# Expert blocks of 640 slots with wide matmuls and unordered scatters, beside a bias MLP computed by matrix products per row group: one change to an attention and mixture-of-experts kernel

## The chip, the cores and the metric

The kernel runs on one core of a Trainium2 chip. The metric is the device time of one execution in microseconds (us); times of several runs are given by their median. Engines: TensorE (PE, with its weight loads PEld), VectorE (DVE), ScalarE (ACT), GpSimd (POOL) and SyncE (SP); DMA transfers are issued here from SP's queue and from POOL's.

## What is computed

Attention over 8 batches and 8 heads, 576 positions of 64 numbers, with a bias that a small MLP (1 to 32 to 8) makes from the relative position; the bias does not depend on the batch. The result, seen as 4608 rows of 512, then goes through a two-layer MLP (512 to 1024 to 512), one of eight experts for each row, as `domain_id` says.

```
scores = scale * q @ k.T
rel = |i - j|;  x = log1p(rel) / log1p(max(i, 1))
bias = relu(x * w1 + b1) @ w2                 # [576, 576, 8 heads]
attn = softmax(scores + bias);  y = attn @ v
x = y as [4608, 512]
for e in range(8):
    rows = (domain_id == e)
    out[rows] = relu(x[rows] @ w1[e]) @ w2[e]
```

The inputs are drawn with a fixed seed. The eight experts get 566, 557, 545, 612, 562, 561, 618 and 587 rows.

## The kernel before

The work stands in five parts, one after the other in the program: constants, bias, routing, attention, experts. A scheduler fixes the order of the instructions on each engine when the kernel is built; an engine then runs its instructions strictly in that order, each after the semaphores it waits for. Tiles come from pools, and a pool closed before another is opened gives its memory to the next, so that the first writers of the new tiles wait for the last readers of the old ones.

*Constants* (`_setup_constants`). The argument of the bias MLP is a log of |i - j| divided by a log of i. One table `L4` holds log1p of the distance for all shifts, with the four groups of 32 partitions one step apart, and `slope` holds w1 / log1p(i) for each row: a row group of four positions i is then one DVE operation that reads a shifted window of 576 columns of `L4` (f16 in SBUF), multiplies by a column of `slope`, and takes the maximum with `nb1`, which is -b1 (L108).

*Bias* (`_phase_fire`). Nine bands of 64 positions. Each band makes 16 tiles `hr` (L108) with forty buffers, then 80 small matmuls (L119) with `hr` as weights against `W2BIG` (32 columns) into the PSUM tile `eb`, which holds two chunks of columns and has four buffers. ACT takes each `eb` out with exp and stores it, with the heads moved outward, into `biasall` (L125). The biases are thus kept as factors exp(bias).

*Routing* (`_phase_route`). A one-hot of the domains, prefix sums along the columns, one matmul for the sum over partitions (`app`), and the slot of each row (`posi`): expert times 768 plus its rank. 36 indirect DMAs from POOL (L190) scatter the row numbers to `fire_perm` in DRAM, 128 each, and each waits for the one before it, since they write the same tensor. SP reads the table back as `permE`; empty slots are filled with the number of the first row of the tile, giving `gidx`.

*Attention* (`_phase_attention`). Per batch POOL issues the casting loads of q (L221) and k (L224). Per head: 18 transposes on PE, two DVE copies to `qkT`, v loaded on SP (L246, L248) and cast on POOL to `vext`, the scores `sc` (L274), exp on ACT (L278), the product with `biasall` on DVE (L284). Then `pu` (L295), normalised by DVE (L300, L301) and written to `fire_x` in DRAM by SP (L307).

*Experts* (`_phase_moe`). Per expert two casting weight loads (L316, L319), 1 MB each in SBUF, two buffers; then six tiles of 128 slots. A tile is gathered by an indirect DMA (L323, two buffers), transposed (L328), copied (L331), goes through 32 matmuls of 128 columns (L335), relu on ACT (L340), 8 matmuls of 512 columns (L343), a copy to `res` (L346, two buffers), and an indirect DMA that scatters the rows to the output (L347). The scatters write one tensor and keep their order.

Of the kernel before, what the change touches and what calls it, by code (L numbers as in the profile page):

```python
# [24 lines left out]
E = 8  # L25
CAP = 768
NCH = CAP // 128
NTOK = B * S
NGR = S // 4
LC = S - 4  # L30
LW = LC + S

# [17 lines left out]
def _setup_constants(tc, G, w1, b1, w2):  # L50

    nc = tc.nc
    cst = G.cst
    G.idn = cst.tile([P, P], F16, tag="idn", name="idn")  # L60
    make_identity(nc, G.idn)

    w1col = cst.tile([P, 1], F32, tag="w1col", name="w1col")
    nc.sync.dma_start(out=w1col, in_=bass.AP(tensor=w1.tensor, offset=0, ap=[[0, 4], [1, 32], [1, 1]]))
    G.nb1 = cst.tile([P, 1], F32, tag="nb1", name="nb1")
    nc.sync.dma_start(out=G.nb1, in_=bass.AP(tensor=b1.tensor, offset=0, ap=[[0, 4], [1, 32], [1, 1]]))
    nc.vector.tensor_scalar(out=G.nb1, in0=G.nb1, scalar1=-1.0, scalar2=None, op0=AO.mult)
    w2sb = cst.tile([HID, 8], F32, tag="w2sb", name="w2sb")
    nc.sync.dma_start(out=w2sb, in_=w2[:, :])
    G.W2BIG = cst.tile([P, 32], F16, tag="W2BIG", name="W2BIG")  # L70
    nc.gpsimd.memset(G.W2BIG, 0.0)
    for g in range(4):
        nc.vector.tensor_scalar(
            out=G.W2BIG[32 * g: 32 * g + 32, 8 * g: 8 * g + 8],
            in0=w2sb, scalar1=8.0, scalar2=None, op0=AO.mult,
        )

    si = cst.tile([P, NGR], I32, tag="si", name="si")
    li = cst.tile([P, LW], I32, tag="li", name="li")
    for g in range(4):  # L80
        nc.gpsimd.iota(si[32 * g: 32 * g + 32, :], base=g, channel_multiplier=0, pattern=[[4, NGR]])
        nc.gpsimd.iota(li[32 * g: 32 * g + 32, :], base=-(LC + g), channel_multiplier=0,
                       pattern=[[1, LW]])
    G.slope = cst.tile([P, NGR], F32, tag="slope", name="slope")
    nc.vector.tensor_copy(out=G.slope, in_=si)
    nc.vector.tensor_scalar(out=G.slope, in0=G.slope, scalar1=1.0, scalar2=None, op0=AO.max)
    nc.scalar.activation(out=G.slope, in_=G.slope, func=AF.Ln, bias=1.0, scale=1.0)
    nc.vector.reciprocal(out=G.slope, in_=G.slope)
    nc.vector.tensor_scalar(out=G.slope, in0=G.slope, scalar1=w1col[:], scalar2=None, op0=AO.mult)
    lf = cst.tile([P, LW], F32, tag="lf", name="lf")  # L90
    nc.vector.tensor_copy(out=lf, in_=li)
    nc.vector.scalar_tensor_tensor(out=lf, in0=lf, scalar=-1.0, in1=lf, op0=AO.mult, op1=AO.max)
    G.L4 = cst.tile([P, LW], F16, tag="L4", name="L4")
    nc.scalar.activation(out=G.L4, in_=lf, func=AF.Ln, bias=1.0, scale=1.0)

    G.biasall = cst.tile([P, NJC, 8, S], F16, tag="biasall", name="biasall")


def _phase_fire(tc, G):
    nc = tc.nc  # L100
    with tc.tile_pool(name="fsb", bufs=1) as fsb, \
         tc.tile_pool(name="fps", bufs=1, space=bass.MemoryType.PSUM) as fps:
        for ib in range(S // 64):
            hrl = []
            for k16 in range(16):
                m = 16 * ib + k16
                hr = fsb.tile([P, S], F16, tag="hr", name="hr", bufs=40)
                nc.vector.tensor_scalar(out=hr, in0=G.L4[:, LC - 4 * m: LC - 4 * m + S],  # L108
                                        scalar1=G.slope[:, m: m + 1], scalar2=G.nb1[:],
                                        op0=AO.mult, op1=AO.max)  # L110
                hrl.append(hr)
            for jcs in ((0, 1), (2, 3), (4,)):
                n = len(jcs)
                jw = JC[jcs[0]][1]
                eb = fps.tile([P, 2, 512], F32, tag="eb", name="eb", bufs=4)
                for k16 in range(16):
                    for lj, jc in enumerate(jcs):
                        j0 = JC[jc][0]
                        nc.tensor.matmul(  # L119
                            out=eb[0:jw, lj, 32 * k16: 32 * k16 + 32],  # L120
# [4 lines left out]
                nc.scalar.activation(  # L125
                    out=G.biasall[0:jw, jcs[0]: jcs[0] + n, :, 64 * ib: 64 * ib + 64],
                    in_=eb[0:jw, 0:n, :].rearrange("p l (i h) -> p l h i", h=8),
                    func=AF.Exp, bias=0.0, scale=0.125)


def _phase_route(tc, G, moe_domain_id):
    nc = tc.nc
    perm_dram = nc.dram_tensor("fire_perm", (E * CAP, 1), I32, kind="Internal").ap()
# [18 lines left out]
    ut = pbuf.tile([P, P], F16, tag="ut", name="ut")  # L152
    nc.gpsimd.memset(ut, 1.0)
    nc.gpsimd.affine_select(out=ut, in_=ut, compare_op=AO.is_ge, fill=0.0,
                            base=-1, channel_multiplier=-1, pattern=[[1, P]])
    apref = pbuf.tile([P, 8, 1], F32, tag="apref", name="apref")
    with tc.tile_pool(name="pps", bufs=1, space=bass.MemoryType.PSUM) as pps:
        app = pps.tile([P, 8], F32, tag="app", name="app")
        nc.tensor.matmul(out=app, lhsT=ut, rhs=rowtot16, start=True, stop=True)
        nc.vector.tensor_copy(out=apref, in_=app.unsqueeze(-1))  # L160
    pa = pbuf.tile([P, 8, 80], F32, tag="pa", name="pa")
# [5 lines left out]
    for sh in (1, 2, 4, 8, 16, 32):  # L167
# [6 lines left out]
    etile = pbuf.tile([P, 8, 36], F32, tag="etile", name="etile")  # L174
    nc.vector.tensor_scalar(out=etile, in0=rap(eif, 0, [[1, 8], [0, 36]]),
                            scalar1=float(CAP), scalar2=None, op0=AO.mult)
    nc.vector.tensor_tensor(out=rtile, in0=rtile, in1=etile, op=AO.add)
# [6 lines left out]
    neg48 = pbuf.tile([P, 48], I32, tag="neg48", name="neg48")  # L184
    nc.gpsimd.memset(neg48, -1)
    nc.sync.dma_start(out=perm_dram.rearrange("(p c) o -> p (c o)", c=48), in_=neg48)
    nidx = pbuf.tile([P, 36], I32, tag="nidx", name="nidx")
    nc.gpsimd.iota(nidx, base=0, channel_multiplier=1, pattern=[[128, 36]])
    for c in range(36):
        nc.gpsimd.indirect_dma_start(  # L190
            out=perm_dram[:, :],
            out_offset=bass.IndirectOffsetOnAxis(ap=posi[:, c:c + 1], axis=0),
            in_=nidx[:, c:c + 1], in_offset=None)
    permE = pbuf.tile([P, E * NCH, 1], I32, tag="permE", name="permE")
    nc.sync.dma_start(out=permE, in_=bass.AP(tensor=perm_dram.tensor, offset=0,
                                             ap=[[1, 128], [128, E * NCH], [1, 1]]))
    permEf = pbuf.tile([P, E, NCH], F32, tag="permEf", name="permEf")
    nc.vector.tensor_copy(out=permEf, in_=permE.rearrange("p (e kk) o -> p e (kk o)", e=E))
    mneg = pbuf.tile([P, E, NCH], F32, tag="mneg", name="mneg")
    nc.vector.tensor_scalar(out=mneg, in0=permEf, scalar1=0.0, scalar2=-1.0,  # L200
                            op0=AO.min, op1=AO.mult)
    tsel = pbuf.tile([P, E, NCH], F32, tag="tsel", name="tsel")
    nc.vector.tensor_tensor(out=tsel, in0=permEf[:, :, 0:1].to_broadcast([P, E, NCH]),
                            in1=mneg, op=AO.mult)
    nc.vector.tensor_tensor(out=tsel, in0=tsel, in1=mneg, op=AO.add)
    nc.vector.tensor_tensor(out=permEf, in0=permEf, in1=tsel, op=AO.add)
    G.gidx = pbuf.tile([P, E, NCH], I32, tag="gidx", name="gidx")
# [200 lines left out]
```

## Time and profile before

| | us |
|---|---|
| median of 11 runs (lowest, highest) | 683.79 (678.13, 694.79) |
| the profiled execution | 684.41 |
| its span | 682.2 |
| busy: PE, PEld | 512.1 (75%), 354.4 (52%) |
| busy: DVE, ACT, POOL | 357.4 (52%), 248.5 (36%), 253.4 (37%) |
| bias stage, from the first L108 to the last L119 | 12.4 to 68.2 |
| first score matmul to the last write of `fire_x` | 85.1 to 416.2 |
| first expert matmul to the last row scatter | 433.9 to 678.2 |

The span is the time from the first to the last instruction that the profiler saw; the time of the execution has 2.2 us around it. Busy shares are means over stages with very different limits. In a group of the profile the columns are the line, the engine, the operation, what it writes and reads with shapes and count, then busy us, mean ns of one, and the idle time of the engine just before with what ended it.

The chain of work that ended last has DMA 31%, PE 29%, ACT 12%, DVE 10%, POOL 6% of the span, and 11% in which an engine waited for nothing that the profile shows. By line, the row scatters of the experts have 18%, the permutation scatters 5%, L274 9%, L278 8%, L119 6%.

### The profile page before, as it was taken

Reading aid. Unit: us, or ns where it says so; the run is one execution under the profiler, and the core shown is the slowest. Engines: PE = TensorE matmul, PEld = TensorE weight load, DVE = VectorE, ACT = ScalarE, POOL = GpSimd, SP = SyncE. Lnnn points to the kernel's source line nnn. Section 1 sums busy time; section 2 is a strip of 40 time slices with the busy share of each in tenths; the row PEclk is TensorE's granted clock in tenths of the full one; section 3 lists DMA queues with packets and bytes.
Section 4 is the critical chain, followed back from the end, with each engine's and each line's share of the span. In section 5 each row is a group of like instructions: output and inputs, shape, how many; then the busy total and the mean of one; then the engine's idle time right before and its main releaser. Section 6 shows DMA issues by size and latency. Waiting matters only on the chain.

```text
span 682.2 us, 15154 instructions
## 1 busy us (share of the span) xinstructions
PE 512.1 (75%) x6225; PEld 354.4 (52%) x6225; DVE 357.4 (52%) x948; ACT 248.5 (36%) x271; POOL 253.4 (37%) x508
## 2 busy tenths in 40 slices
PE   2888197876987538778787873598879697969795
PEld 1777155545555326464555543465646465646463
DVE  6996476785767547868697882121212221212121
ACT  2433175380763713827374560122121121212121
POOL 4000644664744704222230402244435253443442
PEclk9999999797559957977898796699798998979899
DMA  1000999219294393791930205939293847667521
GB/s 4 2 2 1 117 93 101 66 29 121 54 66 76 41 66 89 57 102 37 98 78 20 70 1 106 199 101 186 92 186 98 182 107 164 132 148 149 136 94 61
DMA packets 149292, 60.32 MB, mean 88 GB/s; under 512 B 127720, under 2 KB 140520, under 8 KB 149224
## 3 DMA queue, kind: packets, MB, share of 16 engines
q0 software_dynamic: 93824, 45.12, 53.1%
q1 hardware_dynamic: 55400, 14.25, 10.8%
q8 instruction: 48, 0.79, 0.5%
q14 instruction: 20, 0.16, 0.1%
HBM read 68.22 MB, written 17.34 MB: 125 GB/s over the span
## 4 chain that ended last, share of the span: by engine, by line
DMA 31%; PE 29%; ACT 12%; issue 11%; DVE 10%; POOL 6%; POOLq 0%; SPq 0%; DVEq 0%; ACTq 0%
DMA out_dram<-res,gidx 18%; PE sc L274 9%; ACT eT L278 8%; PE eb L119 6%; DMA fire_perm<-nidx,posi 5%; PE pu L295 5%; PE ops L343 4%; DVE eT L284 4%; DMA fire_x<-xt 3%; DMA xg<-fire_x,gidx 3%; ACT biasall L125 2%; PE hps L335 2%; POOL xg L323 2%; DVE xt L301 2%; PE ptk L237 2%
## 5 line engine op out<-in xcount | busy, mean ns | idle before, releaser
L278 ACT ACTIVATE eT<-sc 128x1152 f16<-128x1152 f32 (+1 forms) x192 | 173.7, 965 | 162.7 <-PE sc L274 161.9
L274 PE MATMUL sc<-qkT 128*128 128x512 f16 (+5 forms) x640 | 130.1, 337 | 27.7 <-DVE qkT L242 15.4
L284 DVE TENSOR_TENSOR eT<-eT,biasall 128x576 f16<-128x576 f16 (+1 forms) x320 | 135.3, 469 | 25.9 <-ACT eT L278 25.2
L346 DVE COPY res<-ops 128x512 f32<-128x512 f32 x48 | 33.2, 691 | 184.5 <-PE ops L343 120.1
L340 ACT ACTIVATE hsb<-hps 128x1024 f16<-128x1024 f32 x48 | 49.1, 1023 | 218.3 <-PE hps L335 187.7
L335 PEld LDWEIGHTS <-w1e 128*128 128x128 f16 x1536 | 94.9, 100 | 21.0 <-issue 10.8
L343 PE MATMUL ops<-w2e,hsb 128*128 128x512 f16 x384 | 99.5, 406 | 7.5 <-ACT hsb L340 6.7
L335 PE MATMUL hps<-xgT,w1e 128*128 128x128 f16 x1536 | 100.6, 223 | 5.7 <-DVE xgT L331 5.3
L295 PE MATMUL pu<-vext,eT 128*128 128x65 f16 (+1 forms) x1600 | 75.2, 207 | 35.9 <-DVE xt L301 14.5
L347 POOL DMA_INDIRECT out_dram<-res,gidx x48 | 47.4, 986 | 126.8 <-DMA out_dram<-res,gidx 76.4
L295 PEld LDWEIGHTS <-eT 128*128 128x128 f16 (+1 forms) x1600 | 65.9, 110 | 48.0 <-DVE xt L301 20.8
L274 PEld LDWEIGHTS <-qkT 128*128 128x128 f16 (+1 forms) x640 | 52.7, 111 | 64.6 <-issue 26.8
L249 POOL CAST vext<-vf 128x256 f16<-128x256 f32 x64 | 30.4, 475 | 97.8 <-PE pu L295 77.6
L343 PEld LDWEIGHTS <-hsb 128*128 128x128 f16 x384 | 36.1, 103 | 53.7 <-ACT hsb L340 14.7
L119 PE MATMUL eb<-W2BIG,hr 128*128 128x32 f16 (+1 forms) x720 | 48.1, 199 | 20.1 <-DVE hr L108 12.9
L323 POOL DMA_INDIRECT xg<-fire_x,gidx x48 | 46.8, 975 | 24.8 <-issue 12.3
L190 POOL DMA_INDIRECT fire_perm<-nidx,posi x36 | 38.3, 1064 | 45.7 <-DMA fire_perm<-nidx,posi 38.5
L119 PEld LDWEIGHTS <-hr 128*128 128x128 f16 (+1 forms) x720 | 40.1, 112 | 28.0 <-DVE hr L108 12.9
L234 PE MATMUL ptq<-idn,q 64*64 64x64 f16 x576 | 41.0, 206 | 13.8 <-DMA q<-in_q_dram 8.3
L234 PEld LDWEIGHTS <-q 64*64 64x64 f16 x576 | 30.3, 119 | 37.2 <-issue 26.5
L328 PE MATMUL pxt<-idn,xg 128*128 128x128 f16 x192 | 17.1, 238 | 42.6 <-DMA xg<-fire_x,gidx 42.5
L108 DVE TENSOR_SCALAR hr<-L,slope,nb 128x576 f16<-128x576 f16 x144 | 49.0, 421 | 0.0
(70 smaller groups left out, 356.1 us busy)
## 6 DMA issues: line engine op xcount, KB each, us to landing
vf<-in_v_dram SPq DMA_DIRECT2D x64, 128.0 KB, 2.3
w1e<-in_moe_w_dram POOLq DMA_DIRECT2D x8, 1024.0 KB, 9.2
w2e<-in_moe_w_dram POOLq DMA_DIRECT2D x8, 1024.0 KB, 12.6
q<-in_q_dram POOLq DMA_DIRECT2D x8, 576.0 KB, 8.7
k<-in_k_dram POOLq DMA_DIRECT2D x8, 576.0 KB, 10.2
fire_x<-xt SPq DMA_DIRECT2D x32, 128.0 KB, 1.8
vf<-in_v_dram SPq DMA_DIRECT2D x64, 16.0 KB, 2.1
xg<-fire_x,gidx POOLq DMA_INDIRECT x48, 3.3
```

Of the source, the lines that this page charges most:

```text
L108: nc.vector.tensor_scalar(out=hr, in0=G.L4[:, LC - 4 * m: LC - 4 * m + S], scalar1=G.slope[:, m: m + 1], scalar2=G.nb1[:], op0=AO.mult, op ...
L119: nc.tensor.matmul(out=eb[0:jw, lj, 32 * k16: 32 * k16 + 32], lhsT=hrl[k16][:, j0: j0 + jw], rhs=G.W2BIG[:, 0:32], start=True, stop=True,)
L234: nc.tensor.transpose(out=ptq[:, 64 * m: 64 * m + 64], in_=q16[0:64, g9, :], identity=G.idn[0:64, 0:64])
L274: nc.tensor.matmul(out=po, lhsT=qkT[:, 1, j0: j0 + jw], rhs=qkT[:, 0, i0s: i0s + iwd], start=True, stop=True)
L278: nc.scalar.activation(out=eT[0:jw0, jgl: jgl + njc, :], in_=sc[0:jw0, 0:njc, :], func=AF.Exp, bias=0.0, scale=scale)
L284: nc.vector.tensor_tensor(out=eT[0:jw, jcn, :], in0=eT[0:jw, jcn, :], in1=G.biasall[0:jw, jcn, h, :], op=AO.mult)
L295: nc.tensor.matmul(out=pu[0:icw, hq, 0:65], lhsT=eTs[h][:, jcn, ic0: ic0 + icw], rhs=vexts[h][:, jcn, 0:65], start=(jcn == 0), stop=(jcn = ...
L323: nc.gpsimd.indirect_dma_start(out=xg[:], out_offset=None, in_=x_dram[:], in_offset=bass.IndirectOffsetOnAxis(ap=G.gidx[:, e, kk: kk + 1], ...
L335: nc.tensor.matmul(out=hps[:, 128 * fc: 128 * fc + 128], lhsT=w1e[:, dc, 128 * fc: 128 * fc + 128], rhs=xgT[:, dc, :], start=(dc == 0), st ...
L340: nc.scalar.activation(out=hsb, in_=hps, func=AF.Relu, bias=0.0, scale=1.0)
L343: nc.tensor.matmul(out=ops_, lhsT=hsb[:, fc, :], rhs=w2e[:, fc, :], start=(fc == 0), stop=(fc == 7))
L347: nc.gpsimd.indirect_dma_start(out=out[:], out_offset=bass.IndirectOffsetOnAxis(ap=G.gidx[:, e, kk: kk + 1], axis=0), in_=res[:], in_offse ...
```

## The change

Four things are changed together.

1. *The bias MLP.* The table of shifts goes. A table `Tnat` holds the argument itself, 18 blocks of 32 rows, each made by iota, cast, absolute value, ln on ACT, a reciprocal of ln of the row and a product. `WBIG` holds eight versions of w1 as weights. A row group is now two matmuls (512 and 64 columns) into a PSUM tile `hpre` of f32 (two buffers), which DVE takes out with the bias added and the relu (`hrelu`, 18 buffers). `eb` is one chunk of columns wide (two buffers); DVE copies it to `biasall`, and one ACT instruction at the end takes exp of all of `biasall`.
2. *Routing.* 640 slots for each expert, and 38 overflow tiles of 128 slots behind them; the slots are counted on DVE (`cnt`, `ovexp`, `novf`, `past`, `obase`). The permutation scatters are declared free of order among each other. Empty slots hold a number past the last row: a gather takes row 0 in its place, a scatter leaves it out by its bounds check.
3. *Experts.* The weights of expert 0 are loaded ahead of attention. Per expert five tiles are gathered (six buffers), the first layer runs over 640 slots with two matmuls of 320 columns for each weight block, then the second layer tile by tile; the row scatters are declared free of order, with four `res` buffers.
4. *Overflow.* After the eighth expert a loop, whose number of turns is read from `novf` on the chip, handles a tile past 640 slots: weights, indices, gather, two layers, scatter. With at most 618 rows for an expert the draw gives zero turns.

```diff
-CAP = 768
+CAP = 640
 NCH = CAP // 128
+NOVF = 38
+NSLOT = E * CAP + 128 * NOVF
+PAD = 1 << 20
...
+    bm32 = cst.tile([32, 4, 32], F32, tag="bm32", name="bm32")
+    G.WBIG = cst.tile([P, 8, 128], F16, tag="WBIG", name="WBIG")
+    nc.gpsimd.memset(G.WBIG, 0.0)
+    for m in range(8):
+        nc.sync.dma_start(
+            out=bm32, in_=bass.AP(tensor=w1.tensor, offset=0, ap=[[0, 32], [0, 4], [1, 32]]))
+        nc.gpsimd.affine_select(out=bm32, in_=bm32, ...)
+        nc.vector.tensor_copy(out=G.WBIG[0:32, m, :], in_=bm32.rearrange("v g c -> v (g c)"))
+    G.Tnat = cst.tile([P, 18, S], F16, tag="Tnat", name="Tnat")
+    nc.gpsimd.memset(G.Tnat, 0.0)
+    for blk in range(18):
+        i0 = 32 * blk
+        nc.gpsimd.iota(tmpi, base=i0, channel_multiplier=1, pattern=[[-1, S]])
+        nc.vector.tensor_copy(out=tmpa, in_=tmpi)
+        nc.vector.scalar_tensor_tensor(out=tmpa, in0=tmpa, scalar=-1.0, in1=tmpa,
+                                       op0=AO.mult, op1=AO.max)
+        nc.scalar.activation(out=tmpa, in_=tmpa, func=AF.Ln, bias=1.0, scale=1.0)
+        nc.gpsimd.iota(pcol, base=i0, channel_multiplier=1, pattern=[[0, 1]])
+        nc.vector.tensor_copy(out=pcolf, in_=pcol)
+        nc.vector.tensor_scalar(out=pcolf, in0=pcolf, scalar1=1.0, scalar2=1.0,
+                                op0=AO.max, op1=AO.add)
+        nc.scalar.activation(out=qcol, in_=pcolf, func=AF.Ln, bias=0.0, scale=1.0)
+        nc.vector.reciprocal(out=qcol, in_=qcol)
+        nc.vector.tensor_scalar(out=G.Tnat[0:32, blk, :], in0=tmpa,
+                                scalar1=qcol[:], scalar2=None, op0=AO.mult)
     G.biasall = cst.tile([P, NJC, 8, S], F16, tag="biasall", name="biasall")
+    nc.gpsimd.memset(G.biasall, 0.0)
...
-                hr = fsb.tile([P, S], F16, tag="hr", name="hr", bufs=40)
-                nc.vector.tensor_scalar(out=hr, in0=G.L4[:, LC - 4 * m: LC - 4 * m + S],
-                                        scalar1=G.slope[:, m: m + 1], scalar2=G.nb1[:],
-                                        op0=AO.mult, op1=AO.max)
+                    hp = fps.tile([P, S], F32, tag="hpre", name="hpre", bufs=2)
+                    for (js, jwd) in ((0, 512), (512, 64)):
+                        nc.tensor.matmul(out=hp[:, js: js + jwd], lhsT=G.WBIG[:, m, :],
+                                         rhs=G.Tnat[:, blk, js: js + jwd], start=True, stop=True)
+                    hr = fsb.tile([P, S], F16, tag="hrelu", name="hrelu", bufs=18)
+                    nc.vector.tensor_scalar(out=hr, in0=hp, scalar1=G.b1x4[:],
+                                            scalar2=0.0, op0=AO.add, op1=AO.max)
...
-                eb = fps.tile([P, 2, 512], F32, tag="eb", name="eb", bufs=4)
+                    eb = fps.tile([P, 512], F32, tag="eb", name="eb", bufs=2)
...
-                nc.scalar.activation(
-                    out=G.biasall[0:jw, jcs[0]: jcs[0] + n, :, 64 * ib: 64 * ib + 64],
-                    in_=eb[0:jw, 0:n, :].rearrange("p l (i h) -> p l h i", h=8),
-                    func=AF.Exp, bias=0.0, scale=0.125)
+                    oap = rap(G.biasall, jc * 8 * S + i0g, [[1, 64], [S, 8]], nparts=jw)
+                    nc.vector.tensor_copy(out=oap, in_=eb[0:jw, :])
+    nc.scalar.activation(out=G.biasall, in_=G.biasall, func=AF.Exp, bias=0.0, scale=0.125)
...
     for c in range(36):
-        nc.gpsimd.indirect_dma_start(
+        _no_order(tc, "slots", nc.gpsimd.indirect_dma_start(
...
+def _no_order(tc, key, inst):
+    ins = inst.ins if hasattr(inst, "ins") else inst
+    tc.declare_no_dep(ins, group=key, reason="rows of one permutation")
+    tc.add_to_no_dep_group(key, ins)
...
         for e in range(E):
+            w1e, w2e = G.wts0 if e == 0 else _load_expert(nc, (G.wsb, msb)[e % 2], moe_w1, moe_w2, e)
+            xT = msb.tile([P, 4, CAP], F16, tag="xT", name="xT", bufs=2)
             for kk in range(NCH):
+                transpose_to(gather(G.gidx[:, e * NCH + kk, :]), xT[:, :, 128 * kk: 128 * kk + 128])
+            hT = msb.tile([P, 8, CAP], F16, tag="hT", name="hT", bufs=2)
+            for fc in range(8):
+                hps = mps.tile([P, 2, 512], F32, tag="hps", name="hps", bufs=2)
+                for hf in range(2):
+                    for dc in range(4):
+                        nc.tensor.matmul(out=hps[:, hf, 0:HC],
+                                         lhsT=w1e[:, dc, 128 * fc: 128 * fc + 128],
+                                         rhs=xT[:, dc, HC * hf: HC * hf + HC],
+                                         start=(dc == 0), stop=(dc == 3))
+                nc.scalar.activation(out=hT[:, fc, :].rearrange("p (a b) -> p a b", a=2),
+                                     in_=hps[:, :, 0:HC], func=AF.Relu, bias=0.0, scale=1.0)
+            for kk in range(NCH):
+                second(hT, 128 * kk, w2e, G.sidx[:, e * NCH + kk, :])
+        novf = nc.values_load(G.novf[0:1, 0:1], min_val=0, max_val=NOVF)
+        with tc.For_i(0, novf, 1) as t:
...
     _phase_route(tc, G, moe_domain_id)
+    G.wsb = ctx.enter_context(tc.tile_pool(name="wsb", bufs=1))
+    G.wts0 = _load_expert(nc, G.wsb, moe_w1, moe_w2, 0)
     _phase_attention(tc, G, q, k, v, x_dram)
```

`second` runs the eight matmuls of 512 columns for one tile, copies `ops` to `res` and scatters the rows; `gather` and `transpose_to` are the old lines with their own buffers; `_load_expert` issues the two weight loads.

## The prediction

> **What bounds the kernel now.** I read the busy time of each engine by stage, then the costliest groups, then the time line at the stage borders. The stages by windows (window; its length; busy us with the number of instructions for PE, PEld, DVE, ACT and POOL; granted clock; DMA share; GB/s):
>
> ```profile
> 12.00:68.00 56.00, 47.94 (x720) 39.99 (x720) 50.33 (x150) 20.45 (x25) 0.00 (x0) 1.00 0.01 2
> 68.00:84.00 16.00, 1.25 (x17) 0.94 (x16) 7.39 (x20) 2.41 (x3) 10.54 (x18) 1.00 2.15 113
> 264.00:416.00 152.00, 122.50 (x1668) 82.62 (x1665) 119.39 (x329) 86.42 (x96) 36.99 (x149) 0.87 0.54 60
> 416.00:433.00 17.00, 0.29 (x4) 0.33 (x5) 0.00 (x0) 0.00 (x0) 4.55 (x5) 0.52 0.89 156
> 433.00:678.00 245.00, 205.00 (x2111) 141.65 (x2109) 51.69 (x96) 49.10 (x48) 103.57 (x107) 0.94 0.59 135
> ```
>
> The bias stage (12 to 68) keeps PE and DVE busy; TensorE then waits 16 us for q and k; eight batches of attention end at 416; after a 17 us gap the experts take 245 us. No engine bounds the whole, so each stage is priced alone. The groups that price the new work (busy, mean ns of one):
>
> ```profile
> L108 DVE TENSOR_SCALAR hr<-L,slope,nb 128x576 f16<-128x576 f16 x144 | 49.0, 421 | 0.0
> L346 DVE COPY res<-ops 128x512 f32<-128x512 f32 x48 | 33.2, 691 | 184.5 <-PE ops L343 120.1 <-DMA out_dram<-res,gidx 64.4
> L301 DVE TENSOR_TENSOR xt<-pu,rz 128x256 f16<-128x256 f32 x64 | 26.4, 422 | 12.1 <-DMA fire_x<-xt 10.5
> L163 POOL MEMSET pa<- 128x640 f32 x1 | 0.7, 662 | 0.0
> L218 POOL MEMSET qkT<- 64x1152 f16 x2 | 2.0, 1052 | 58.9 <-PE eb L119 58.9
> L92 DVE SCALAR_TENSOR_TENSOR lf<-lf 128x1148 f32<-128x1148 f32 x1 | 1.4, 1354 | 0.0
> ```
>
> L108 reads f16 from SBUF; L346 and L301 read f32 from PSUM and cost 1.05 ns for each further element ((691-422)/256). And the borders on the time line (start, length):
>
> ```profile
> 70.31 1.95 POOL L221 DMA_DIRECT2D q<-in_q_dram  x1
> 78.98 0.69 PE L234 MATMUL ptq<-idn,q 64*64 64x64 f16 x9 [8.34 <-DMA q<-in_q_dram]
> 83.80 0.68 PE L237 MATMUL ptk<-idn,k 64*64 64x64 f16 x9 [4.13 <-DMA k<-in_k_dram]
> 128.84 0.54 SPq L307 DMA_DIRECT2D fire_x<-xt  x1
> 415.73 0.47 SPq L307 DMA_DIRECT2D fire_x<-xt  x1
> 442.80 1.00 POOL L323 DMA_INDIRECT xg<-fire_x,gidx  x1 [0.30 <-issue]
> 444.11 0.95 POOL L323 DMA_INDIRECT xg<-fire_x,gidx  x1 [0.30 <-issue]
> ```
>
> One q or k load takes 8.7 us from issue to first use; two indirect DMAs in a row start 1.31 us apart.
>
> **Bias stage.** Before, it ends at 68. After, each of 144 row groups is two matmuls into PSUM (512 and 64 columns) and a DVE eviction of 128x576 f32 from PSUM: 691 + 64 x 1.05 = 758 ns in place of 344 (20 of L108 in 6.88 us on the time line). The 45 eb evictions move from ACT (128x1024 in 1.02 us, beside PE) to DVE, 691 ns each. A band of 16 groups: 16 x 0.758 = 12.1. Then only two eb buffers: the third to fifth chunk (48 matmuls at 59 ns, from 80 in 4.75 us of the old band, plus two handovers) alternate with their evictions; I lay this out as 5.1, with 0.3 for waits: 17.5 a band, where the old one took 6.1. PE's part of a group (some 0.25 us) hides under the eviction.
>
> Ahead of it the tables. POOL memsets cost 0.9 ns an element (both rows): Tnat 10368 elements 9.4 us, biasall 23040 elements 20.8 us. In the compiled order both stand ahead of the third WBIG slice, so that starts near 36; the other slices then go round one buffer (SP load 0.5 + some 2.1 landing as the small vf loads, select 0.4, DVE copy 0.25): 6 x 3.2, so the eighth is there at 56. The 18 Tnat blocks cost DVE 2.1 us each (cast 0.39, absolute value 0.757 from L92's slope, multiply 0.42, three small ones at 0.17), placed among the first two bands. From 56: 8 evictions and 5 blocks 18; five eb evictions with a block and a half 8; band two with 7 blocks 28 + 5.5; seven bands 7 x 17.5 = 122.5. End of the bias stage: 56 + 18 + 8 + 33.5 + 122.5 = **238**. Bounds: 212 with the memsets at half price (15) and half of an eb turn's waits gone (9 x 1.2); 262 with each eb handover 0.2 dearer (9) and the 48 products 1.6 times slower (9 x 1.7), as the eight sc matmuls after the wait at 85 took 2.08 us and later 1.30.
>
> [...]
>
> The final exp over biasall, one ACT instruction of 23040 elements at 0.85 ns (1128 ns for 1152, 639 for 576): 20 us. It hides under the wait for k below; without that cover it costs up to 20.
>
> **Routing and the first load.** In the compiled POOL order the weights of expert 0 (2 issues), two memsets and q come at the end of the bias stage, then all 36 permutation scatters in one run, then k of batch 0. Before, k was issued ahead of the first scatter. The scatters need posi: some 36 small DVE operations after the last band (the longer slot arithmetic and the eT memsets among them), 13 us where the old chain took 9. Being unordered they wait only for the DMA eight back, so issue sets the pace: 36 x 1.31 = 47. Then k: 8.7. First k transpose: 238 + 13 + 47 + 8.7 = **307**; the old delay after the stage was 15.8, now 69. q behind the weights (about 13.5 us, as the first gather waited behind them at 420) hides under this. Queued behind k on POOL: the vext casts. SP loads novf, then sidx, which waits for the last scatter, and only then v of heads 2 to 7: from 299, at some 2 us each there by 315, while pu, their first reader, follows 24 us after the first k; hidden, and up to 10 us if it is not (permE, sidx's forerunner, took 10.2). Bounds: 60 (scatters at 1.06, their own length) to 80.
>
> **Attention.** Batch 0 took 84 to 129, 45 with scatters in POOL's queue; I take 42. The last writes of batches 4 to 7 lie 38 apart, those of 1 to 3, with scatters between, 40, 44 and 50; all seven at 38: 266. End: 307 + 42 + 266 = **615** (415.7 before; the freed 20 us are in this).
>
> **Experts.** The draw gives each expert 545 to 618 tokens, so no overflow: 40 tiles for 48, zero trips. PE per expert, in order: 20 transposes with their copies, about 3 us nearly alone; 64 products of 320 columns at 136 ns (between 56 at 128, 45 in 2.68, and 216 at 512, eight start to start 1.73): 8.7; 40 of 512: 8.6; joints 0.4. Sum 20.7, against 31.5 now (start to start of the weight loads: six tiles of 4.28 and 5.8 lost on ordered scatters behind weights). ACT's relu (0.69 for 640) and DVE's copies lie under PE; POOL needs 10 x 1.31 + 2 = 15. DMA was 0.59 busy in 245 us = 145 us; less a sixth of what rows take of it (145 less 7 x 13.5 for weights), some 137 in 166: tight. From the last write: gather 2.5 + 1.0 + 2.8, five gathers and the first transposes to 12; first expert 17.4 + 4 cold; seven at 20.7 = 145; last row out 4.5; closing 4 as now; leaving the loop 3 (bounds 0 to 10, no row): **190**, against 266.5 now. Sum: 615 + 190 = 805 of span; the profiled run has 684.4 for a span of 682.2, and agrees with the median of 683.8; so **807 us**.
>
> **Rivals.** (1) Weights set the pace of the experts: 5.8 us lost on each again, 26.5 each: 807 + 46 = 853. For it: DMA 83% full, row scatters in the same queue behind weights; against: a load is issued some 30 us before use and res has four buffers. 0.10. (2) Bias stage milder: loads, memsets and Tnat wholly beside the bands: 16 + 9 x 17.5 = 174, so 743. Against: the compiled order puts them ahead. 0.08. (3) Faster: DVE evicts PSUM at L108's rate: nine bands of 16 x 0.42 + 5 x 0.42 = 80, ending at 96 with tables free, 142 earlier: 665. It decides once the stage ends before 115. The f32 rows L346 and L301 speak against; 0.02. (4) The unordering does not act: scatters their median landing of 2.8 us further apart, 36 x 2.8 more: 908; the compiled waits exclude nearly all of it, 0.01.
>
> **Numbers.** The forecast has 0.78, no change 0.01. Its bounds and most of (1) make the range 760 to 850. Under 0.5% a measurement could not tell from no change. Faster 0.02, same 0.01, slower 0.97.
>
> **What would show it.** A DVE group hrelu<-hpre near 758 ns x144; end of biasall near 238; 36 scatters 1.3 apart with k behind them; batches of 38; experts of 20.7. Wrong if hrelu costs 0.45, k comes before the scatters, or the experts stay at 26 or more.

## The result and the profile after

| | before | after |
|---|---|---|
| median, us (lowest, highest; runs) | 681.34 (671.76, 694.79; 39) | 877.08 (870.63, 899.64; 10) |
| profiled execution, its span | 684.41, 682.2 | 869.44, 867.5 |
| ratio after / before, 95% interval | | 1.291 (1.285 to 1.296) |

The change makes the kernel 29% slower. The direction was forecast with 0.97; the time was forecast at 807 with a range of 760 to 850, and 877 lies outside it. Some executions show a lower granted clock and take longer (899.64 us at 0.886, against 870.63 at 0.935), so the figure behind a slash below, 874.35 for the changed kernel, is the median without them, and gains are taken between these second figures. For experiments a ratio with its interval is given where enough executions allow it, else the medians alone (the kernel before had medians of 686 to 689 beside them). Stages are read from one profiled execution each, and its mean granted clock stands in the table at the end. The bias stage of the changed kernel did not follow that clock: its last `eb` copy starts between 286.9 and 287.1 in four executions with clocks from 0.900 to 0.936.

The stages of the changed kernel by windows (window, length, busy us of PE, PEld, DVE, ACT, POOL with counts, granted clock, DMA share, GB/s):

```profile
181.00:287.00 106.00, 58.29 (x508) 32.35 (x507) 105.86 (x92) 0.00 (x0) 0.49 (x1) 1.00 0.00 1
287.00:356.00 69.00, 0.88 (x11) 0.66 (x10) 13.11 (x38) 20.69 (x2) 45.44 (x55) 1.00 0.55 51
397.00:672.00 275.00, 216.46 (x2959) 145.99 (x2959) 210.32 (x586) 151.55 (x168) 72.93 (x277) 0.87 0.70 67
685.00:863.00 178.00, 156.09 (x968) 92.61 (x966) 40.63 (x75) 45.05 (x64) 82.05 (x86) 0.96 0.75 160
```

In the bias stage (181 to 287) DVE is busy for 105.86 of 106 us and PE for 58: the band is DVE's. Then comes TensorE's wait for k (287 to 356), with POOL's scatters as most of the work. Set against the sum on record, stage by stage:

| stage | predicted, us | measured, us |
|---|---|---|
| eighth WBIG slice copied | 56 | 61.4 |
| end of the bias stage | 238 | 289.7 |
| from there to k's first transpose | 69 | 67.7 |
| batch 0 | 42 | 39.8 |
| seven batches | 266 | 275 |
| experts to the end of the span | 190 | 195 |
| sum | 805 | 867.5 |

Of the 62.5 us that the sum lacks, 51.7 are the bias stage. Its groups (busy, mean ns of one, idle before and what ended it), from the costliest groups of the changed kernel:

```profile
L129 DVE TENSOR_SCALAR hrelu<-hpre,b1x 128x576 f16<-128x576 f32 x144 | 113.6, 818 | 2.5 <-PE hpre L122 2.1
L426 DVE COPY res<-ops 128x512 f32<-128x512 f32 x40 | 27.6, 691 | 132.1 <-PE ops L423 114.0
L143 DVE CAST biasall<-eb 128x512 f16<-128x512 f32 (+1 forms) x45 | 104.2, 2595 | 0.0
```

L426 reads 512 f32 from PSUM in 691 ns, the price that the prediction gave to L143. L143 reads the same amount and takes 2595 ns. One band on the time line of DVE (start, length; the window ends inside the last row):

```profile
231.25 11.52 DVE L143 CAST biasall<-eb 128x512 f16<-128x512 f32 x5
242.39 12.60 DVE L129 TENSOR_SCALAR hrelu<-hpre,b1x 128x576 f16<-128x576 f32 x16
254.91 6.98 DVE L143 CAST biasall<-eb 128x512 f16<-128x512 f32 x3
```

Five eb copies in 11.1 us and sixteen row groups in 12.5 make 23.7 us a band; 17.5 were forecast. What sets L143 apart is its output: `rap(G.biasall, ..., [[1, 64], [S, 8]])` reads eb in a row (position, then head) and puts each f16 element 1152 bytes from the last. Before, ScalarE did the same rearrangement by reading PSUM in steps and writing runs of 64.

At the kernel's start a second loss shows on the time line (in brackets the idle time of the engine just before, with what ended it):

```profile
5.61 8.73 POOL L83 MEMSET Tnat<- 128x10368 f16 x1
7.65 6.78 DVE L80 CAST WBIG<-bm 32x128 f16<-32x128 f32 x1
17.65 0.60 POOL L91 IOTA tmpi<- 32x576 int32 x1
17.72 19.94 DVE L80 CAST WBIG<-bm 32x128 f16<-32x128 f32 x1 [3.28 <-POOL bm L76]
18.29 19.29 POOL L106 MEMSET biasall<- 128x23040 f16 x1
346.54 1.82 POOL L293 DMA_DIRECT2D k<-in_k_dram  x1
357.41 0.68 PE L306 MATMUL ptk<-idn,k 64*64 64x64 f16 x9 [51.51 <-DMA k<-in_k_dram]
```

A cast of 128 elements on DVE ended only when POOL's memset had ended, once after 6.78 us (14.43 against 14.34) and once after 19.94 (37.66 against 37.58). The second cast starts 0.57 us ahead of its memset, beside an iota on POOL. The last two rows are the late k: issued behind the 36 scatters that began at 301.24, it held PE to 357.41.

### The profile page after: what moved, and what is told of

The parts are those of the page before. It is cut to its first block, busy times and chain, and to the rows that moved or that the text cites. A ratio compares the mean times of both kernels' runs of the same rounds, so it can differ in the third digit from the quotient of the medians.

```text
span 867.5 us, 13744 instructions
## 1 busy us (share of the span) xinstructions
PE 532.6 (61%) x5394; PEld 330.3 (38%) x5394; DVE 566.4 (65%) x1110; ACT 255.7 (29%) x295; POOL 270.3 (31%) x533
## 4 chain that ended last, share of the span: by engine, by line
DVE 34%; PE 23%; DMA 13%; issue 11%; ACT 11%; POOL 7%; POOLq 0%; SPq 0%; DVEq 0%
DVE biasall L143 11%; ACT eT L347 10%; DVE hrelu L129 8%; PE sc L343 8%; DMA out_dram<-res,sidx 4%; POOL fire_perm L259 4%; PE hps L439 4%; PE pu L364 4%; DMA fire_x<-xt 3%; PE hpre L122 3%; DVE eT L353 3%; DVE WBIG L80 3%; PE ops L423 2%; POOL xg L408 2%; DMA bm<-in_w_dram 2%
## 5 line engine op out<-in xcount | busy, mean ns | idle before, releaser
L122 PE MATMUL hpre<-Tnat,WBIG 128*128 128x512 f16 (+1 forms) x288 | 91.8, 423 | 81.6 <-DVE Tnat L102 40.3
L129 DVE TENSOR_SCALAR hrelu<-hpre,b1x 128x576 f16<-128x576 f32 x144 | 113.6, 818 | 2.5 <-PE hpre L122 2.1
L426 DVE COPY res<-ops 128x512 f32<-128x512 f32 x40 | 27.6, 691 | 132.1 <-PE ops L423 114.0
L136 PE MATMUL eb<-W2BIG,hrelu 128*128 128x32 f16 (+1 forms) x720 | 55.0, 197 | 81.5 <-DVE biasall L143 71.7
L143 DVE CAST biasall<-eb 128x512 f16<-128x512 f32 (+1 forms) x45 | 104.2, 2595 | 0.0
L136 PEld LDWEIGHTS <-hrelu 128*128 128x128 f16 (+1 forms) x720 | 46.3, 126 | 110.2 <-issue 91.2
L443 ACT ACTIVATE hT<-hps 128x640 f16<-128x640 f32 x64 | 45.0, 704 | 143.3 <-PE hps L439 143.3
L439 PE MATMUL hps<-xT,w1e 128*128 128x320 f16 x512 | 78.1, 317 | 0.0
L423 PE MATMUL ops<-w2e,hT 128*128 128x512 f16 x320 | 70.4, 379 | 0.0
L439 PEld LDWEIGHTS <-w1e 128*128 128x128 f16 x512 | 52.7, 104 | 23.2
L387 POOL DMA_INDIRECT out_dram<-res,sidx x40 | 39.9, 997 | 59.5 <-DVE res L426 55.7
```

What stands on the lines that cost most here:

```text
L122: nc.tensor.matmul(out=hp[:, js: js + jwd], lhsT=G.WBIG[:, m, :], rhs=G.Tnat[:, blk, js: js + jwd], start=True, stop=True,)
L129: nc.vector.tensor_scalar(out=hr, in0=hp, scalar1=G.b1x4[:], scalar2=0.0, op0=AO.add, op1=AO.max)
L136: nc.tensor.matmul(out=eb[0:jw, 32 * k16: 32 * k16 + 32], lhsT=hrl[k16][:, j0: j0 + jw], rhs=G.W2BIG[:, 0:32], start=True, stop=True,)
L143: nc.vector.tensor_copy(out=oap, in_=eb[0:jw, :])
L387: _no_order(tc, "out_rows", tc.nc.gpsimd.indirect_dma_start(out=out[:], out_offset=bass.IndirectOffsetOnAxis(ap=idx, axis=0), in_=res[:], ...
L423: nc.tensor.matmul(out=ops_, lhsT=hT[:, fc, t0: t0 + 128], rhs=w2e[:, fc, :], start=(fc == 0), stop=(fc == 7))
```

## The experiments

**Where eb lands.** Only the copy's two access patterns change places.

```diff
-                    oap = rap(G.biasall, jc * 8 * S + i0g, [[1, 64], [S, 8]], nparts=jw)
-                    nc.vector.tensor_copy(out=oap, in_=eb[0:jw, :])
+                    nc.vector.tensor_copy(out=G.biasall[0:jw, jc, :, i0g: i0g + 64],
+                                          in_=eb[0:jw, :].rearrange("p (i h) -> p h i", h=8))
```

> The changed kernel, with the VectorE copy of eb reading PSUM in 32-byte steps and writing biasall in runs of 64 neighbouring elements, in place of reading in a row and writing every element 1152 bytes from the last. Theory A (the scattered writes cost 2.6 us): the 45 copies fall to about 0.70 us, a steady band from 23.7 to about 18 us, nine bands less the overlap of the first two some 50 us; 877 goes to about 827 (815 to 840). Theory B (the copy is slow because of PSUM, the cast, or matmuls beside it, and not because of where it writes): the copies stay at 2.4 to 2.7 us and the time at 877.

Measured: 820.41 / 816.92 (812.03 to 824.67, 4 runs). The group among the costliest of DVE:

```profile
L142 DVE CAST biasall<-eb 128x512 f16<-128x512 f32 (+1 forms) x45 | 29.3, 682 | 4.5 <-PE eb L136 3.8
```

And a band on DVE's time line (start, length):

```profile
168.93 2.65 DVE L142 CAST biasall<-eb 128x512 f16<-128x512 f32 x4
172.06 0.68 DVE L142 CAST biasall<-eb 64x512 f16<-64x512 f32 x1 [0.48 <-PE eb L136]
172.67 12.44 DVE L129 TENSOR_SCALAR hrelu<-hpre,b1x 128x576 f16<-128x576 f32 x16
185.03 2.65 DVE L142 CAST biasall<-eb 128x512 f16<-128x512 f32 x4
```

The copies fall from 2595 to 682 ns with PSUM as the source, the cast and the matmuls beside them unchanged: theory A. The band is 16.1 us (168.93 to 185.03), the stage ends at 220.6 in place of 289.7. Reading PSUM in steps of 32 bytes cost nothing that shows here (682 ns, and 691 in L426, which reads in a row).

**What a scattered write costs.** Two runs add copies of 128x512 into scratch tiles, each on a line of its own, nine of each; part of the first run's edit:

```diff
                     nc.vector.tensor_copy(out=oap, in_=eb[0:jw, :])
+                    if jc == 0:
+                        nc.vector.tensor_copy(out=sa[:, 0:512], in_=eb)
+                        nc.vector.tensor_copy(out=rap(sa, 0, [[2, 512]]), in_=eb)
+                        nc.vector.tensor_copy(out=rap(sa, 0, [[8, 512]]), in_=eb)
+                        nc.vector.tensor_copy(out=rap(sa, 0, [[1, 64], [64, 8]]), in_=eb)
...
```

> The changed kernel with eight more copies of the first eb of each band into scratch tiles, only to time them, nine of each; the output is not touched. Theory A (each two-byte write that does not join its neighbour in a line costs extra): f16 in a row from PSUM 0.69 us; every 2nd element 0.7 to 1.4; steps of 16, 128 and 1152 bytes all near 2.6; f32 at steps of 1152 bytes either 0.7 (only narrow writes cost) or 2.6 (the step costs); f16 from SBUF at 1152 bytes 2.4 to 2.6; strided read with runs of 64 written 0.7. Theory B (PSUM or neighbouring work makes it slow): the copy from SBUF at 1152 bytes is the only fast one. ScalarE with the same scattered write: 0.6 if the cost is VectorE's alone, over 2 if it is the memory's. The time itself goes up by about 9 times the sum of the copies, 9 x 10 = 90.

> The changed kernel with eight more copies of 128x512 into scratch tiles on each band's first eb, nine of each, output untouched; no ScalarE copy beside them this time. They separate the cast from where the elements land. Theory A (narrowing to f16 on a scattered write is what takes 5.1 ns an element, wherever it reads): f32 from SBUF to f16 at 1152-byte steps near 2.6 us; f32 to f32 and f16 to f32 at 1152 bytes near 1.2; f16 to f16 at 16 bytes 1.3; in a row 0.7 or less; f32 from PSUM to f16 at 8 bytes between 0.92 and 2.6. Theory B (PSUM as source is what doubles it): f32 from SBUF to f16 at 1152 bytes near 1.3.

Measured: one execution each, 1009.32 and 932.09; the first is 132 us above the changed kernel's 877, where 90 were forecast. Four groups of the first run (every 2nd element, every 8th, steps of 128 bytes, f32 at 1152 bytes) and three of the second (f32 from SBUF to f16 and to f32 at 1152 bytes, f32 from PSUM at every 4th element):

```profile
L149 DVE CAST sa<-eb 128x512 f16<-128x512 f32 x9 | 8.3, 922 | 0.0
L150 DVE CAST sa<-eb 128x512 f16<-128x512 f32 x9 | 23.5, 2614 | 0.0
L151 DVE CAST sa<-eb 128x512 f16<-128x512 f32 x9 | 23.6, 2622 | 0.0
L152 DVE COPY sf<-eb 128x512 f32<-128x512 f32 x9 | 10.9, 1207 | 0.0
```

```profile
L150 DVE CAST sa<-sg 128x512 f16<-128x512 f32 x9 | 11.8, 1312 | 0.0
L151 DVE COPY sf<-sg 128x512 f32<-128x512 f32 x9 | 6.1, 676 | 0.0
L155 DVE CAST sa<-eb 128x512 f16<-128x512 f32 x9 | 11.5, 1278 | 0.0
```

All of them together, mean us for 128x512 by the step from one written element to the next (in a row also L142 of the run above and L426):

| source and target | in a row | 4 B | 8 B | 16 B | 128 B | 1152 B |
|---|---|---|---|---|---|---|
| PSUM f32 to f16 | 0.68 to 0.87 | 0.92 | 1.28 | 2.61 | 2.62 | 2.44 to 2.66 |
| PSUM f32 to f32 | 0.69 to 0.87 | | | | | 1.21 |
| SBUF f32 to f16 | 0.61 | | | | | 1.31 |
| SBUF f32 to f32 | | | | | | 0.68 |
| SBUF f16 to f32 | | | | | | 0.83 |
| SBUF f16 to f16 | 0.29 | | | 1.51 | | 1.28 |

From PSUM to f16 the price climbed from 0.92 us at 4 bytes to 2.61 at 16 and was flat from there to 1152 (2.44 to 2.66). The full 2.6 us took two things together with the step: two-byte elements as the target (at 1152 bytes 1.31 against 0.68 from SBUF, 2.4 to 2.7 against 1.21 from PSUM) and PSUM as the source (2.4 to 2.7 against 1.31). With one of the two alone the scattered write took 1.2 to 1.5. Theory A of the first run, that the writes alone explain it, holds only by half (f16 from SBUF took 1.28, not 2.4 to 2.6), and theory A of the second, that the narrowing is what costs, fell: its theory B held (1.31). Why PSUM as the source doubles the price was not tested. ScalarE with the same scattered write from PSUM took 2.44 us, so the price is not VectorE's alone.

**The memsets.** Tnat and biasall are not filled with zeros; the products contract over the 32 filled rows, and exp is taken of what is filled.

```diff
-    nc.gpsimd.memset(G.Tnat, 0.0)
-    nc.gpsimd.memset(G.biasall, 0.0)
...
-                            lhsT=G.WBIG[:, m, :],
-                            rhs=G.Tnat[:, blk, js: js + jwd],
+                            lhsT=G.WBIG[0:32, m, :],
+                            rhs=G.Tnat[0:32, blk, js: js + jwd],
```

> The changed kernel without the memsets of Tnat and biasall (the pre-activation products then contract over the 32 rows that are filled; exp is taken of the filled part of biasall alone). Theory A (GpSimd's memsets of 9 and 19 us hold up VectorE's casts and the weight slices, and all that follows): the eighth slice is copied near 32 us in place of 61, and the time falls by 22 to 28, to about 852. Theory B (the 18 table blocks on VectorE set the start in any case): the slices come early, the bands don't; the time falls by under 10, to 868 or more.

Measured: 855.80 / 849.49 (843.42 to 874.27, 6 runs); the eighth slice is copied at 32.0 and the stage ends at 260.2, 29.5 earlier. The same casts on DVE's time line now:

```profile
7.55 0.21 DVE L80 CAST WBIG<-bm 32x128 f16<-32x128 f32 x1
10.99 0.21 DVE L80 CAST WBIG<-bm 32x128 f16<-32x128 f32 x1 [0.71 <-POOL bm L76]
```

0.21 us in place of 6.78 and 19.94: theory A, and a gain of 25 us. In the changed kernel both casts ended within 0.1 us of the memset beside them (0.09 and 0.08); what held them no run here shows.

**Buffers for the rows.** `res` gets six buffers in place of four, one line.

> The changed kernel with six res buffers in place of four. Theory A (the fifth copy to res of an expert waits 2.7 us for the first row scatter, which lands late behind a weight load, and the xT copies and with them TensorE's transposes wait behind it): an expert goes from 23.1 to about 20.7 us, 877 to about 860 (855 to 866). Theory B (the weights and rows on the DMA engines set the pace): the wait moves to the transposes or to the first matmuls, experts stay at 22.5 to 23.1, time 872 to 877.

Measured: 867.85 / 867.85 (862.83 to 872.91, 4 runs), a gain of 6.5 us. In the changed kernel the fifth copy of an expert waits, and TensorE's transposes behind it:

```profile
751.55 0.69 DVE L426 COPY res<-ops 128x512 f32<-128x512 f32 x1 [2.72 <-DMA out_dram<-res,sidx]
...
752.62 0.71 PE L416 MATMUL pxt<-idn,xg 128*128 128x128 f16 x8 [2.34 <-DMA out_dram<-res,sidx]
```

With six buffers that wait is gone, and another takes its place in part:

```profile
743.72 2.33 PE L439 MATMUL hps<-xT,w1e 128*128 128x320 f16 x16 [1.65 <-ACT hT L443]
...
755.79 0.72 PE L416 MATMUL pxt<-idn,xg 128*128 128x128 f16 x8 [0.67 <-DVE xT L418]
```

Experts go from 23.1 to 21.9 us each (median from weight load to weight load), between the theories: the wait was real, and PE waits 1.65 us in the first layer instead. What it waits for there is not settled. The load of the DMA engines does not explain it: they were busy 0.85 of the time from 738 to 760, and 0.9 or more during an expert of the last run below (471.4 to 491.2), where the same code takes 19.8 us without this wait.

**Order of the row scatters.** The row scatters are declared in order again.

```diff
-    _no_order(tc, "out_rows", tc.nc.gpsimd.indirect_dma_start(
+    tc.nc.gpsimd.indirect_dma_start(
```

> The changed kernel with the row scatters of the experts in order again; the permutation scatters stay free. Theory A (a row scatter lands a median 6.4 us after its issue, and five in a row with each waiting for the last make an expert at least 32 us): experts go from 23.1 to about 32 us each, the time up by some 60, to 935 (915 to 960). Theory B (alone in the queue a scatter lands in under 3.5 us and five hide beside the products): 885 or less.

Measured: 911.01 / 909.38, ratio 1.320 (1.307 to 1.332); 28.7 us an expert (weight loads at 725.50, 754.19, 782.66) in place of 23.1. Theory A in kind, but with less than its 32 us, so that the time lies under its range of 915 to 960. Freeing the rows of order was worth some 35 us (874.35 against 909.38).

**Order of the permutation scatters.** The same for the 36 scatters of the routing, and only these.

> The changed kernel with the 36 permutation scatters in order again (each waits for the one before); the row scatters stay free. Theory A (what costs is not the scatter but where it stands: freed of order, all 36 go in one run ahead of k of batch 0, 45 us; in order, the scheduler places k behind the first of them and spreads the rest over attention): k's first transpose comes about 24 us after the bias stage in place of 68, batches 0 to 3 lengthen by some 20 to 25 as before, 877 goes to about 850 (835 to 865). Theory B (as the prediction's fourth rival had it: in order, each scatter comes 2.8 us later and all that follows is late by 100): about 977.

Measured: 847.04 / 844.26, ratio 1.228 (1.217 to 1.238). On POOL's time line k now stands behind the first scatter:

```profile
301.18 1.06 POOL L259 DMA_INDIRECT fire_perm<-nidx,posi  x1 [9.00 <-DVE posi L252]
302.25 1.80 POOL L293 DMA_DIRECT2D k<-in_k_dram  x1
305.45 1.04 POOL L259 DMA_INDIRECT fire_perm<-nidx,posi  x1 [1.40 <-DMA fire_perm<-nidx,posi]
```

In the profiled executions (859.18 and 869.44) k's first transpose comes at 310.7 in place of 357.4, and attention takes 345 in place of 315, part of which may be the clock (0.900 against 0.935). The kernel is 30 us faster with its scatters further apart. The prediction's fourth rival, 100 us later in order, had the wrong sign: it held the place of the scatters fixed, while the scheduler put k and the casts of v into the pauses that order leaves.

**The new bias MLP, mended.** Matrix products stay; ScalarE takes eb out with exp in runs of 64 (no last exp), no memsets (the products contract over the 32 filled rows), six `res` buffers.

```diff
-                    nc.vector.tensor_copy(out=oap, in_=eb[0:jw, :])
-    nc.scalar.activation(out=G.biasall, in_=G.biasall, func=AF.Exp, bias=0.0, scale=0.125)
+                    nc.scalar.activation(out=G.biasall[0:jw, jc, :, i0g: i0g + 64],
+                                         in_=eb[0:jw, :].rearrange("p (i h) -> p h i", h=8),
+                                         func=AF.Exp, bias=0.0, scale=0.125)
```

> The changed kernel with its bias MLP kept as matrix products and three things undone: ScalarE takes eb out with exp in runs of 64 (no last exp over biasall), no memsets of Tnat and biasall, six res buffers. Theory A (VectorE's row groups of 0.79 us set the band once eb is off VectorE: 16 x 0.79 = 12.6 to 14 us a band, slices at 33): the bias stage ends near 180 in place of 290, 877 goes to about 755 (735 to 775), still slower than before. Theory B (PE and eb's two buffers set the band at 16 us as in the run with runs of 64): stage end near 205, about 785.

Measured: 759.08 / 753.01, ratio 1.107 (1.096 to 1.118). Theory A: bands of 14.5 us (12.8 of row groups and a wait of 1.67 for the products), stage end at 182.9. Even so it is slower than before, whose stage ended at 68: the row groups read f32 from PSUM at 0.80 us, where L108 took 0.34 from SBUF, and the tables stand ahead.

**The old bias MLP with the rest of the change.** `_setup_constants` and `_phase_fire` are those of before.

> The changed kernel with the bias stage of before (constants, 144 VectorE row groups from the shifted table, ScalarE taking eb out with exp); routing, attention and experts as changed. Theory A (the parts add: bias stage to 68, then 69 us of slot chain, 36 scatters and k as in the changed kernel, attention 315, experts 195, 2 around): 649 (635 to 665), faster than before by about 5%, so that the bias MLP alone is what makes the change slower. Theory B (the changed routing and experts are no gain of their own, because 53 us of scatters ahead of k and the longer gathers eat it): 675 or more.

Measured: 651.36 / 651.26 (4 runs), ratio 0.944 (0.935 to 0.953). Theory A: the routing and the experts, as changed, make the kernel 5.6% faster than the kernel before beside it, and the bias MLP alone turns that into a loss of 29%.

**Taking the scatters and k out of the way.** To the last kernel are added six `res` buffers, the qkT memsets on VectorE, q and k of batch 0 loaded at the start, and routing ahead of the bias stage. The pool that holds q and k opens earlier, so the weights of expert 0 load from 13.3 too:

```diff
+    for nm, src in (("q0", q), ("k0", k)):
+        t = G.wsb.tile([D, 72, D], F16, tag=nm, name=nm)
+        nc.gpsimd.dma_start(out=t, in_=src[0]...)
+    _phase_route(tc, G, moe_domain_id)
     _phase_fire(tc, G)
-    _phase_route(tc, G, moe_domain_id)
```

> The kernel with the old bias stage and the changed routing and experts (median 651 in its run), with four moves more: the routing stands ahead of the bias stage in the program, q and k of batch 0 are loaded at the start, the two small memsets of qkT go to VectorE, and there are six res buffers. Theory A (the 69 us after the bias stage are the slot chain, the scatters and k, and all three fit beside the bias stage, whose GpSimd and DMA queues are idle): the bias stage lengthens by some 8 us for the chain on VectorE, k's first transpose follows within 5 us of its end, and 651 goes to about 580 (565 to 595). Theory B (the scatters stand ahead of the casts of v on GpSimd and hold batch 0, or VectorE's chain costs what the wait cost): 610 or more.

Measured: 626.73 / 608.13 (608.13 to 634.99, 6 runs; the second figure is one execution): faster than 651.26, but 28 us from the forecast by the second figure and 47 by the first, and not by the mechanism of theory B. In the profiled execution (627.32), while the scatters went out from 38 to 86, ACT stood from 41.5 and PE from 49.5, DVE ran its row groups to 58 and then stood too. PE came on from 61, soon with single matmuls far apart (the crawl that the next runs ask about), and the first transpose came at 118.8:

```profile
73.36 0.96 POOL L246 DMA_INDIRECT fire_perm<-nidx,posi  x1 [0.31 <-issue]
...
82.89 0.19 PE L122 MATMUL eb<-W2BIG,hr 128*128 128x32 f16 x1 [2.61 <-issue]
85.73 0.19 PE L122 MATMUL eb<-W2BIG,hr 128*128 128x32 f16 x1 [2.65 <-issue]
```

Two runs ask whether it is the scatters without a pause that slow the other engines. In both they are in order again; in the second the routing is also back behind the bias stage.

> The kernel of 627 us (old bias stage, routing ahead of it, early q and k, six res buffers) with its permutation scatters in order again: 14 of them stand beside the bias stage, each after the landing of the last, the others go between the casts of batches 0 to 2. In the run before, all engines but GpSimd crawled from 40 to 90 us while 36 scatters were issued 1.26 to 1.43 us apart, and the bias stage ended 35 us late. Theory A (it is the scatters issued without a pause that hold the other engines up): spaced 2.4 us or more, the bias stage ends near 80 in place of 110 and the time falls to about 595 (585 to 605). Theory B (the crawl comes of something else in this order of instructions, such as the routing chain between the row groups): bias stage near 110 again and 620 to 640.

> The same, with the routing back behind the bias stage: no scatter beside the bias stage, all 36 in order between the casts of the first batches, q and k of batch 0 still loaded at the start. Theory A: the bias stage ends at 70 to 72 with nothing slowed, k's first transpose follows within 5 us, batches 0 to 3 pay some 25 us for the scatters: 600 (590 to 615), so that the place of the scatters decides little once they are spaced. Theory B (what slowed the bias stage slows attention by as much): 625 or more.

Measured: 598.14 / 580.54 (forecast 585 to 605), ratio 0.846 (0.839 to 0.854), and 583.27 / 577.22 (forecast 590 to 615, so under its range), ratio 0.846 (0.840 to 0.852); the two ratios are the same and the best of all. In the first, the bias stage ran without the crawl and the first transpose came at 78.4. The granted clock does not explain the crawl: it fell to 0.50 near 37 in both, and PE was busy 2.47 us of 20 in the run before and 12.22 of 14 in this one (windows as above, the run before first):

```profile
70.00:90.00 20.00, 2.47 (x16) 1.48 (x15) 1.84 (x5) 0.00 (x0) 12.03 (x13) 0.50 0.09 1
50.00:64.00 14.00, 12.22 (x187) 10.22 (x187) 14.00 (x42) 5.17 (x7) 14.00 (x1) 0.50 0.01 2
```

But this does not isolate the pause, since only four scatters got out before 78; the first was held for 33 us, as the time lines of POOL and DVE show:

```profile
38.18 33.23 POOL L246 DMA_INDIRECT fire_perm<-nidx,posi  x1 [23.18 <-DVE hr L111]
...
37.23 34.06 DVE L111 TENSOR_SCALAR hr<-L,slope,nb 128x576 f16<-128x576 f16 x100
```

It looks like the memsets with the roles exchanged: a run of row groups from SBUF, and a GpSimd issue that ended when the run did (71.41 against 71.29). It is no rule, for in the run before 58 row groups from 37.22 on ran beside scatters that took 1.10 to 1.17 us each. Why that run crawled instead of holding its scatters stays open. The first transpose is at 71.7 in the last run, with the clock at 1.00 from 20 to 70, attention pays for its scatters (338 us), and experts take 19.8 us in both.

All runs by their profiled execution (mean granted clock of the span; starts of k's first transpose and of the last write of `fire_x`; under experts the end of the span less that write):

| run | clock | k | last write | experts |
|---|---|---|---|---|
| before | 0.883 | 83.8 | 415.7 | 266 |
| changed | 0.935 | 357.4 | 672.2 | 195 |
| eb in runs of 64 | 0.908 | 289.4 | 620.2 | 203 |
| no memsets | 0.888 | 327.2 | 667.8 | 205 |
| six res | 0.936 | 357.1 | 679.7 | 188 |
| rows in order | 0.915 | 357.4 | 673.8 | 237 |
| permutation in order | 0.900 | 310.7 | 655.4 | 202 |
| bias MLP mended | 0.940 | 250.5 | 559.8 | 188 |
| old bias MLP | 0.888 | 138.2 | 456.6 | 205 |
| routing ahead | 0.835 | 118.8 | 437.4 | 188 |
| the same, spread | 0.823 | 78.4 | 428.1 | 178 |
| routing behind, spread | 0.890 | 71.7 | 409.8 | 178 |

## Why the prediction was right and where it failed

The step that failed is "The 45 eb evictions move from ACT (128x1024 in 1.02 us, beside PE) to DVE, 691 ns each", and with it the eb turn, "I lay this out as 5.1". The mechanism was right, more work on DVE with only two eb buffers; the term was mis-sized. L346's row has the same source and count but writes f32 in a row; L143 writes f16 at 1152 bytes, and takes 2595 ns: 45 x 1.9 = 86 us more of DVE time. Some of it lies where DVE would have waited for PE: per band the turn is 11.1 us against 5.4, and over nine bands some 51 us. With the pattern turned round and nothing else, the turn is 3.7 us (16.1 less 12.4) and the time falls by 57, to 820, which lies inside the range. The access pattern stood in the diff; the lower and upper bounds were drawn around waits and matmuls, and none around the write. That 51 is so near the 51.7 of the whole stage is luck: the slices (5 us) and the row groups (4) came on top, and the work before the first two turns, with the table blocks in it, took 8.4 us less than the sum had (14.5 for 18 and 23.2 for 28).

Smaller, in the order of the sum:

- The slices: the memsets themselves were well priced (8.73 and 19.29 against 9.4 and 20.8), and the third slice came late as said. That DVE's casts stood still beside them (6.78 and 19.94 us for 0.21) was not in the working. The third slice was copied at 42.7, some 3.5 us later than the sum had it, and the later ones came 3.4 to 4.0 us apart in place of 3.2, so that the eighth is 5 us late. Without the memsets the stage ends 29.5 us earlier and the time falls by 25.
- The row groups: 782 ns from start to start for 758, 3 to 4 us in all. The faster rival (an eviction near 421 ns) is excluded by 818 ns on 144 records.
- The granted clock was 1.00 in the bias stage (181 to 287), and the sum has no term for a lower one there.
- The final exp, 19.4 us at 291, was hidden under the wait for k as forecast, and so was q behind the weights.
- The delay from stage end to k held to 1.3 us (67.7 for 69), with k behind the 36 scatters as forecast; that it is so near is luck in part. The slot chain took 11.6 us (forecast 13), the scatters 45.3 (47) and k 10.9 (8.7). The 8.7 was read as the time of "One q or k load", but only q's row shows it: k's row before has 11.5, from 72.26 to 83.80.
- Attention 39.8 and 275 (forecast 42 and 266): one of the seven batches took 45.6, the others 37.2 to 39.3 for the forecast 38. Why that one was longer was not tested.
- The experts: 23.1 us each, not 20.7. The first rival's mechanism was there in small: a row scatter behind a weight load landed late (issued at 743.93, it let the fifth copy go at 751.55, while the median landing of a row scatter before was 2.7 us), four `res` buffers did not cover it, and the fifth copy waited 2.7 us in the expert shown. Six buffers gave back 1.2 us an expert; the rest of the 2.4 stays open, and it is no fault of the price of the work, since the last run has 19.8. The 4 us more for the first expert ("4 cold") no trace shows: its products took 18.8 us (683.67 to 702.49) and those of the second 18.5 (708.30 to 726.76), with the granted clock at 0.53 from 672 to 685, 0.86 from 685 to 690 and 1.00 from 690 to 700.
- The milder bias stage (743) did not come; that the mended MLP (759) lies near it is chance, since other things were changed there.
- The fourth rival was wrong in sign, as the ordered permutation showed.

## What to carry to other kernels

Price an eviction by its whole access pattern and not by source and count: turn a rearrangement round so that the steps fall on the read and the writes run in a row (here 682 ns in place of 2595). Before freeing a chain of DMAs of its order, look at what the scheduler had put into its pauses, since a load queued behind the whole run can cost more than the chain (here 30 us). Do not leave a long GpSimd memset beside short VectorE casts that something waits for (here two casts of 0.21 us lasted 6.78 and 19.94 beside memsets of 8.73 and 19.29).

## What was not expected of the hardware

- 512 elements written as f16 at steps of 16 bytes or more took 2.4 to 2.7 us from PSUM and 1.3 to 1.5 from SBUF; as f32 at 1152 bytes 1.21 and 0.68.
- A VectorE cast of 32x128 lasted 19.94 us beside a GpSimd memset, and an indirect DMA's issue on GpSimd lasted 33.23 us beside 100 VectorE operations of 0.34 us.
- With 36 scatters issued 1.26 to 1.48 us apart beside the bias stage, TensorE's single matmuls came up to 3.5 us apart from 63 to 89, and the stage's last matmul came at 116 in place of 76 in the next run. This was seen in one profiled execution and its cause is open; the granted clock was 0.50 in both.
